# Gated mix of two attentions on one core: small VectorE jobs of slots 1 to 8 handed to GpSimd and ScalarE, the split of the output weights moved

## The chip, the core and the metric

The kernel runs on one core of a Trainium2 chip. The core has five engines that run their own instruction queues in order: TensorE (PE, with its weight loads as PEld), VectorE (DVE), ScalarE (ACT), GpSimd (POOL) and SyncE (SP), whose queue here issues nearly all DMAs. They meet at semaphores alone. The metric is the device time of one launch in microseconds (us), the median of several runs.

## The reference, cut to what matters

One input x (2048 rows of 512) goes through two attention blocks of 32 heads, 16 wide. Block A is causal within four segments of 512 rows, with a memory that is carried from segment to segment; block B is a full softmax attention over all 2048 rows. A gate from x mixes their outputs row by row.

```python
# A, segment s of 4 (L = 512), per head; g = sigmoid(beta)
p = softmax(qs @ ks.T * scale + mask)
o = g * (phi(qs) @ M) / (phi(qs) @ z + 1e-6) + (1 - g) * (p @ vs)
M, z = M + phi(ks).T @ vs, z + phi(ks).sum()
a = concat(o) @ wo
# B
b = concat(softmax(q @ k.T * scale) @ v) @ wo_b
gate = sigmoid((x * gate_w).sum(-1))
out = gate * a + (1 - gate) * b
```

## The kernel before

A first phase (until the first exponential at 341.0 us) projects x to q, k and v of both blocks, works out A's memory part and leaves all of it in DRAM. The second phase is the attention, and the change lies in it.

A *unit* is one block, four heads and 512 query rows: 32 units of A (u = 0 to 31, in the order `UA`) and 32 of B (u = 32 to 63). The loop of line 1050 runs 32 *slots*; slot k treats units ua = k and ub = 32 + k. A slot has 37 *groups* n = 0 to 36 (`NG`): groups 0 to 31 are B's scores, 32 to 36 A's. Two groups make one *iteration* `it` = n // 2, and the work beside the scores hangs on `it`. The schedule is written by hand: each engine takes its instructions in the order in which the program emits them.

In each group:

- `t_group` (583) makes transposed scores, two matmuls (L598) into two of three PSUM banks (`TB`, `MB`), and two exponentials on ScalarE (L604) into `raw`. For A, GpSimd then masks the diagonal blocks (affine selects, L607).
- `plan` puts the *row maxima* of the next slot's B unit (`s_b`, 528: two matmuls L535 and a VectorE maximum over 128 x 1024, L537) beside the groups, one a group, and those of the next A unit (`s_a`, 503: L513, L517, maxima L521 and L523) beside groups 32 to 36. The maxima read the two `sbk` pairs of banks in turn, so TensorE can be two ahead of VectorE and no more.
- `pvs` (965) adds probabilities times values (`pv`, L620) into the bank `PVB`: B's during groups 2 to 33, A's from group 34 to group 0 of the next slot. When a unit is complete, `fin_copy` (623) copies PVB to `pvs` and stores it: B's in group 33 (ScalarE, L629), A's in group 0 of the next slot (VectorE, L627, for u below 31). The first `pv` of B in group 2 waits for that copy.

Other work of a slot:

- `m_chain(k + 1)` (541) at iteration 10 folds the maxima to 128 x 32 numbers (L546) and splits them into a 16-bit and a rest part `m8`. For k + 1 of 8 to 31 GpSimd does the split (L555 to L558), otherwise VectorE (L560 to L562). `m_rows` (564) behind group 24 turns `m8` by TensorE, ScalarE copies it (`mr`), and SP writes it into rows of q that are used from group 32 on and in the next slot.
- `fin_load`, `fin_rec` (641), `fin_bc`: the sums of a finished unit come back from DRAM as `rec`, VectorE takes reciprocals (L644), they are multiplied by the gates, stored (`rd`) and read back as a broadcast `d`. B's `fin_rec` is at iteration 5, A's at 6. The product is VectorE's (L650, L652) for u % 32 below 7 and for 31 and 63, otherwise GpSimd's (L647, L648, L652).
- `fin_norm` (662): GpSimd multiplies 128 x 512 outputs by `d` (L664), B's at iteration 9, A's at 13, in even slots from 2 on.
- `load_wo` (672): in slots 1 to 4 at iteration 9 SP loads a quarter of both output weights and GpSimd splits it (L676 cast, L677 subtraction, twice each).
- From slot 9 on, output rows (`out_rows`, 700) are multiplied in group 1 and later.

Of the kernel before, what the change touches and what calls it, by code (L numbers as in the profile page):

```python
# [38 lines left out]
def gated_mix_kernel(ctx, tc, xt, wq, wk, wv, wo, beta, wqkv, wob, gate_w, out):  # L39
    nc = tc.nc  # L40
# [426 lines left out]
    def load_q(u):  # L467
        kd, qd, c = UN[u]
        load_qk(q_of(u), kd, 0, qd, c)

    def load_ka(u):
        kd, qd, c = UN[u]
        load_qk(KA[u % 2], kd, 1, qd, c)

    def load_kb(k, c=None):
        dst = KB[k % 3] if c is None else KB[k % 3][:, :, c * C:(c + 1) * C]
        load_qk(dst, "B", 1, k % 8, c)
# [6 lines left out]
    def load_vb(g):  # L484
        v_src(VB[g % 2], "B", g % 4, None)

    def load_va(u):
        kd, qd, c = UN[u]
        v_src(VA[(u // 2) % 2], "A", qd // 2, c)
# [4 lines left out]
    def pair_max(k):  # L494
        if k not in MX:
            MX[k] = W.tile([128, 2, 4, 4], FT, name="mx")
        return MX[k]
# [43 lines left out]
    def m_chain(k):  # L541
        mx = pair_max(k)
        if k == 1:
            nc.vector.memset(mx[:, 0], 0.0)
        if k < 32:
            nc.vector.tensor_reduce(mx[:, 1], MXB.pop(32 + k).rearrange("q j p i c -> q (j p) i c"), axis=AX.X,  # L546
                                    op=OP.max)
        else:
            nc.vector.memset(mx[:, 1], 0.0)
        del MX[k]  # L550
        mx = mx.rearrange("q u h i -> q (u h i)")
        m8 = M8[k] = W.tile([128, 2, 32], FT, name="m8")
        hi = W.tile([128, 32], HF, name="mhi")
        if 8 <= k < 32:
            nc.gpsimd.tensor_scalar(mx, mx, -1.0 / AUX, None, op0=OP.mult)  # L555
            nc.gpsimd.tensor_copy(hi, mx)
            nc.gpsimd.tensor_copy(m8[:, 0], hi)
            nc.gpsimd.tensor_tensor(m8[:, 1], mx, hi, op=OP.subtract)  # L558
        else:
            nc.vector.tensor_scalar(hi, mx, -1.0 / AUX, None, op0=OP.mult)  # L560
            nc.vector.tensor_copy(m8[:, 0], hi)
            nc.vector.scalar_tensor_tensor(m8[:, 1], mx, -1.0 / AUX, hi, op0=OP.mult, op1=OP.subtract)  # L562
# [16 lines left out]
    AT = {}  # L579
# [3 lines left out]
    def t_group(u, n, banks, between=()):  # L583


        kd, qd, c = UN[u]
        bs = [bank(banks) for _ in range(2)]
        c0 = 0
        for it, hs in (((n // 2, (n % 2 * 2, n % 2 * 2 + 1)),) if kd == "B" else GA[n]):
            q0 = 128 * it if kd == "A" else 0  # L590
            w = C - q0
            pn = it if kd == "B" else it % 2
            for j, h in enumerate(hs):
                if j:
                    for f in between:
                        f()
                r = slice(64 * j, 64 * j + 64)
                nc.tensor.matmul(bs[j][:, c0:c0 + w], k_of(u, h // 2)[r, 128 * it:128 * it + 128],  # L598
                                 q_of(u)[r, h // 2, q0:], start=True, stop=True)
                PT[u, it, h] = PTILE[pn % 2][:, 2 + j if (kd, it) == ("A", 2) else h][:, c0:c0 + w]  # L600
            c0 += w
        for j in range(2):
            pt = PTILE[pn % 2][:, 2 + j if (kd, n) == ("A", 4) else hs[j]]
            nc.scalar.activation(pt, bs[j], AF.Exp, scale=AT["esc", kd, qd // 2])  # L604
            if kd == "A":
                m = pt[:, :128] if n < 2 else pt.rearrange("p (a t) -> p a t", a=4)[:, ::3 if n < 4 else 2]
                nc.gpsimd.affine_select(out=m, in_=m, pattern=[[1, 128]] if n < 2 else [[0, 2], [1, 128]],  # L607
                                        compare_op=OP.is_ge, fill=0.0, base=0, channel_multiplier=-1)

    def pv(u, it, lo=0, hi=None):  # L610

        kd, qd, c = UN[u]
        g, q = divmod(qd, 2)
        q0 = 128 * it if kd == "A" else 0
        hi = hi or C - q0
        last = 2 if kd == "A" else NT - 1
        vt = VA[(u // 2) % 2] if kd == "A" else VB[g % 2]
        for h in range(4):
            pt = PT[u, it, h]
            nc.tensor.matmul(PVB[32 * h:32 * h + E + 1, q0 + lo:q0 + hi], vt[:, it, 4 * q + h, :], pt[:, lo:hi],  # L620
                             start=it == 0 and lo == 0, stop=it == last and q0 + hi == C, skip_group_check=True)

    def fin_copy(u):

        ps = W.tile([128, C], FT, name="pvs", bufs=1)
        if u < 31:
            nc.vector.tensor_copy(ps, PVB)  # L627
        else:
            nc.scalar.activation(ps, PVB, AF.Copy)  # L629
        AT["pd", u] = D.tile([4, 32, C], FT, name=f"pd{u}")  # L630
        nc.sync.dma_start(AT["pd", u].rearrange("h r t -> (h r) t"), ps)
# [9 lines left out]
    def fin_rec(u):  # L641
        kd, qd, c = UN[u]
        r = AT.pop(("r", u))
        nc.vector.reciprocal(r, r)  # L644
        early = u % 32 < 7 or u in (31, 63)
        if kd == "A" and not early:
            nc.gpsimd.tensor_scalar(r, r, nq[:, qd:qd + 1], None, op0=OP.mult)  # L647
            nc.gpsimd.tensor_tensor(r, r, grow[:, 0, c], op=OP.mult)  # L648
        elif kd == "A":
            nc.vector.scalar_tensor_tensor(r, r, nq[:, qd:qd + 1], grow[:, 0, c], op0=OP.mult, op1=OP.mult)  # L650
        else:
            (nc.vector if early else nc.gpsimd).tensor_tensor(r, r, grow[:, 1, c], op=OP.mult)  # L652
        AT["rd", u] = D.tile([128, E], FT, name=f"rd{u}")
        nc.sync.dma_start(AT["rd", u], r)
# [16 lines left out]

    def load_wo(g):
        for a, w in enumerate((wo, wob)):
            raw = AT["o"][1][:, g, a]
            nc.sync.dma_start(raw, w[g * 128:(g + 1) * 128, :])
            nc.gpsimd.tensor_copy(AT["wh"][:, g, a], raw)  # L676
            nc.gpsimd.tensor_tensor(AT["wl"][:, g, a], raw, AT["wh"][:, g, a], op=OP.subtract)  # L677

    def o_cols(c, t):
        return AT["o"][c % 2][:, :, :, t * 128:(t + 1) * 128]  # L680
# [139 lines left out]
    for n in range(8):  # L820
        w, c = divmod(n, 4)
# [13 lines left out]
    early = st33[:EARLY]  # L835
# [17 lines left out]
    for blk in range(16):  # L853
        g, c = divmod(blk, 4)
# [110 lines left out]
    def pvs(k, n):  # L965

        ua, ub = k, 32 + k
        if n == 0:
            if k:
                pv(ua - 1, 2)  # L970
                fin_copy(ua - 1)
        elif k == 31 and n < 2 * NT:
            if n % 2 and n > 1:
                pv(ub, n // 2 - 1)
        elif 2 <= n < 2 * NT + 2:
            pv(ub, n // 2 - 1, n % 2 * 256, n % 2 * 256 + 256)
            if n == 2 * NT + 1:
                fin_copy(ub)
        elif n > 2 * NT + 1:
            m = n - 2 * NT - 2  # L980
            if m < 2:
                pv(ua, 0, 256 * m, 256 * m + 256)
            else:
                pv(ua, 1)
                pv(ua, 3)
# [64 lines left out]
    for k in range(32):  # L1050
        ua, ub = k, 32 + k
        banks = T3 + [b[:, 0] for b in SBK] * (k == 31)
        for n in range(NG):
            it = n // 2 if n < NG - 1 else NT + 2
            mid = plan.pop((k, n)) if n < 2 * NT and (k, n) in plan else []
            t_group(*(ub, n) if n < 2 * NT else (ua, n - 2 * NT), banks, mid)
            for f in plan.get((k, n), []) + ex[k][0].get(n, []):
                f()
            pvs(k, n)
            for f in ex[k][1].get(n, []):  # L1060
                f()
            if n % 2 == 0 and n < NG - 1:
                continue
            beside(k, it)
            if it == S_LAST:
                m_chain(k + 1)
            if it == 4 and not k:
                late()
            if it == 4 and not k:
                load_q(ub + 2)  # L1070
                for c in range(NC4):
                    load_kb(2, c)
            if it == NT and k < 29:
                load_q(ub + 3)
                load_kb(k + 3)
            if it == 6 and k < 31:
                load_q(ua + 1)
                load_ka(ua + 1)
                if (ua + 1) % 2 == 0:
                    load_va(ua + 1)  # L1080
            if it == 9:
                if k % 2 == 0 and k < 30:
                    load_vb(k // 2 + 1)
                if 1 <= k <= 4:
                    load_wo(k - 1)
    pv(31, 2)
    fin_copy(31)
    fin_bc(63)
# [13 lines left out]
    for t in range(4):  # L1102
        d = den[:, t * 128:(t + 1) * 128]
        o = o_cols(3, t)[:, 3, 0]
# [36 lines left out]
```

## Time and profile before

| what | before |
|---|---|
| median of 3 runs | 1838.19 us (1837.33 to 1839.88) |
| the profiled execution | 1839.64 us, its span 1837.9 us |
| mean granted TensorE clock | 0.997 |
| VectorE's largest group, maxima of B (L537) | 1172.4 us, 1024 times 1.21 us |
| ScalarE's largest, exponentials (L604, tb and mb) | 884.2 + 469.0 us |
| TensorE's largest, probabilities times values of B (L620) | 645.3 us |

The span runs from the first to the last instruction of the profiled execution. Durations of one instruction include a part that overlaps the next one on the same engine, so a sequence is shorter than the sum of its durations; the steps from start to start say what a sequence costs. A row of the timeline has start and length in us, engine, line of the kernel, operation, names, how many instructions were put together, and in brackets the idle time before it with what ended it. The view by stretches gives busy times between two points of the span.

### The profile page before, as it was taken

The numbers are of one execution on the slowest core, as the hardware profiler recorded it, in microseconds if no ns is written. First come the engines' busy times: TensorE is split into PE (matmuls) and PEld (weight loads), VectorE is DVE, ScalarE is ACT, GpSimd is POOL, SyncE is SP. The second block draws the span as 40 slices with busy tenths as digits, with TensorE's granted clock in tenths as the row PEclk, the third lists the DMA queues.
The fourth block names the chain that finished last, engine by engine and source line by source line (L and its number), as shares of the span: only waits on it lengthen the run. The fifth ranks groups of instructions, "written<-read, shape, count | busy, mean of one in ns | idle before, by whom it ended". The sixth has DMA issues, their size and how long they took to land.

```text
span 1837.9 us, 44287 instructions
## 1 busy us (share of the span) xinstructions
PE 1804.9 (98%) x17781; PEld 729.1 (40%) x17781; DVE 1591.5 (87%) x1772; ACT 1432.5 (78%) x2709; POOL 339.6 (18%) x691
## 2 busy tenths in 40 slices
PE   8999999899999999999999999999999999999998
PEld 6787777522222222333333333333333333333325
DVE  7445786699999999999999999999999999999942
ACT  4233333488989999989898989898989898989894
POOL 6100000101212011212121212121212121212122
PEclk9999999999999999999999999999999999999999
DMA  7554534332323232223232323232323232323111
GB/s 231 118 149 124 152 105 108 77 91 73 92 73 91 62 80 62 80 68 86 68 86 68 86 69 85 68 87 68 85 70 87 68 85 70 87 68 86 47 38 61
DMA packets 162482, 158.92 MB, mean 86 GB/s; under 512 B 40140, under 2 KB 126620, under 8 KB 162276
## 3 DMA queue, kind: packets, MB, share of 16 engines
q1 hardware_dynamic: 158692, 149.29, 29.5%
q0 software_dynamic: 3296, 6.27, 1.8%
q8 instruction: 140, 2.29, 0.6%
q14 instruction: 66, 0.54, 0.1%
q10 hardware_dynamic: 288, 0.52, 0.1%
HBM read 103.38 MB, written 50.86 MB: 84 GB/s over the span
## 4 chain that ended last, share of the span: by engine, by line
PE 78%; DVE 15%; ACT 4%; issue 2%; DMA 1%; ACTq 0%; SPq 0%; DVEq 0%; POOLq 0%
PE pvb L620 28%; DVE mxb L537 12%; PE tb L598 12%; PE sbk L535 9%; PE mb L598 6%; PE tb L311 3%; ACT raw L604 3%; PE mb L311 3%; PE tb L705 2%; PE tb L285 2%; PE sbk L513 2%; PE sbk L285 2%; PE sbk L311 1%; PE mb L705 1%; PE pvb L311 1%
## 5 line engine op out<-in xcount | busy, mean ns | idle before, releaser
L537 DVE TENSOR_REDUCE mxb<-sbk 128x2 f32<-128x1024 f32 x1024 | 1172.4, 1210 | 24.7 <-PE sbk L535 13.1
L604 ACT ACTIVATE raw<-tb 128x512 f32<-128x512 f32 x1555 | 884.2, 600 | 63.7 <-PE tb L598 26.9
L620 PE MATMUL pvb<-raw,vb 128*17 128x256 f32 (+1 forms) x8072 | 645.3, 388 | 0.0
L535 PE MATMUL sbk<-kb,qb 64*128 64x512 f16 x2048 | 553.2, 378 | 9.6 <-DVE mxb L537 8.7
L604 ACT ACTIVATE raw<-mb 128x512 f32<-128x512 f32 x782 | 469.0, 600 | 32.7 <-PE mb L598 16.6
L598 PE MATMUL tb<-qb,kb 64*128 64x512 f16 x1342 | 468.2, 381 | 2.0 <-DVE st L326 1.0
L598 PEld LDWEIGHTS <-kb 64*128 64x128 f16 x2048 | 143.3, 93 | 414.8 <-issue 408.9
L620 PEld LDWEIGHTS pvb<-raw,vb 128*17 128x17 f32 x8072 | 138.0, 95 | 403.3 <-issue 393.9
L598 PE MATMUL mb<-qb,kb 64*128 64x512 f16 x679 | 258.6, 381 | 0.0
L607 POOL TENSOR_SCALAR_AFFINE_SELECT raw<-raw 128x256 f32<-128x256 f32 (+1 forms) x320 | 115.4, 361 | 326.4 <-ACT raw L604 318.0
L535 PEld LDWEIGHTS <-qb 64*128 64x128 f16 x2048 | 137.1, 93 | 43.5 <-issue 33.6
L521 DVE TENSOR_REDUCE mx<-sbk 128x2 f32<-128x1024 f32 (+1 forms) x128 | 133.9, 1087 | 7.2 <-PE sbk L517 6.2
L620 PE MATMUL pvb<-raw,va 128*17 128x256 f32 (+2 forms) x1280 | 103.2, 383 | 3.8 <-ACT pvs L629 1.1
L664 POOL TENSOR_TENSOR o<-o,d 128x512 f32<-128x512 f32 x31 | 39.5, 1273 | 218.9 <-DMA d<-rd 176.3
L523 DVE TENSOR_REDUCE mx<-sbk 128x4 f32<-128x512 f32 x64 | 60.5, 946 | 12.4 <-PE sbk L517 12.4
L513 PE MATMUL sbk<-ka,qa 64*128 64x512 f16 (+3 forms) x512 | 70.7, 296 | 0.0
L323 ACT ACTIVATE st<-tb,rng 128x512 f16<-128x512 f32 x25 | 17.2, 688 | 63.4 <-DVE phi L322 25.6
L598 PE MATMUL tb<-qa,ka 64*128 64x512 f16 (+3 forms) x339 | 61.8, 302 | 0.0
L652 POOL TENSOR_TENSOR rec<-rec,grow 128x16 f32<-128x16 f32 x24 | 5.3, 221 | 276.0 <-DVE rec L644 276.0
L517 PE MATMUL sbk<-cmask,crows 64*128 64x64 bf16 x1024 | 52.8, 189 | 0.0
L517 PEld LDWEIGHTS <-crows 64*128 64x128 bf16 x1024 | 46.5, 94 | 13.7
L323 ACT ACTIVATE st<-mb,rng 128x512 f16<-128x512 f32 x21 | 14.4, 687 | 47.6 <-PE mb L311 19.1
(337 smaller groups left out, 1717.0 us busy)
## 6 DMA issues: line engine op xcount, KB each, us to landing
vb<-vdB SPq DMA_DIRECT2D x16, 1088.0 KB
pd<-pvs SPq DMA_DIRECT2D x64, 256.0 KB
kb<-dB SPq DMA_DIRECT2D x60, 256.0 KB
dB<-st SPq DMA_DIRECT2D x64, 128.0 KB
dA<-st SPq DMA_DIRECT2D x64, 128.0 KB
o<-pd SPq DMA_DIRECT2D x64, 128.0 KB
d<-rd SPq DMA_DIRECT2D x63, 128.0 KB
kb<-dB SPq DMA_DIRECT2D x60, 128.0 KB
```

The costliest lines, as they stand in the source:

```text
L285: nc.tensor.matmul(b, (XH, XL)[xi][c][:, n % 4, tl * 128:(tl + 1) * 128], WV[wi][:, n % 4, :], start=n == 0, stop=n == 11)
L311: nc.tensor.matmul(b, WS[ws][w][wi][:, k, :], (XH, XL)[xi][c][:, k, :], start=n == 0, stop=n == 11)
L513: nc.tensor.matmul(b[:, j, c0:c0 + n], q_of(u)[r, p, i * 128:(i + 1) * 128], k_of(u, p)[r, :n], start=True, stop=False)
L517: nc.tensor.matmul(b[:, j, c0 + n - 128 + w.start:c0 + n - 128 + w.stop], crows[r, n2 - 1], cmask[r, n2 - 1, w], start=False, stop=n2 == 2)
L521: nc.vector.tensor_reduce(m[:, :, p, i], b[:, :, :n], axis=AX.X, op=OP.max)
L523: nc.vector.tensor_reduce(m[:, :, :, i], b.rearrange("q j (p k) -> q j p k", p=2)[:, :, :, :n], axis=AX.X, op=OP.max)
L535: nc.tensor.matmul(b[:, j], q_of(u)[r, p, i * 128:(i + 1) * 128], k_of(u, p)[r, kc * C:(kc + 1) * C], start=True, stop=True)
L537: nc.vector.tensor_reduce(MXB[u][:, :, p, i, kc], b, axis=AX.X, op=OP.max)
L598: nc.tensor.matmul(bs[j][:, c0:c0 + w], k_of(u, h // 2)[r, 128 * it:128 * it + 128], q_of(u)[r, h // 2, q0:], start=True, stop=True)
L604: nc.scalar.activation(pt, bs[j], AF.Exp, scale=AT["esc", kd, qd // 2])
L607: nc.gpsimd.affine_select(out=m, in_=m, pattern=[[1, 128]] if n < 2 else [[0, 2], [1, 128]], compare_op=OP.is_ge, fill=0.0, base=0, channe ...
L620: nc.tensor.matmul(PVB[32 * h:32 * h + E + 1, q0 + lo:q0 + hi], vt[:, it, 4 * q + h, :], pt[:, lo:hi], start=it == 0 and lo == 0, stop=it ...
```

## The change

Four edits, all in the second phase:

- `m_chain`: GpSimd splits the maxima for k of 2 to 31 instead of 8 to 31; new are k = 2 to 7, in slots 1 to 6.
- `fin_copy`: ScalarE copies the sums of A's units 0 to 7 too (group 0 of slots 1 to 8).
- `fin_rec`: GpSimd does the gate products for u % 32 of 1 to 6 too (slots 2 to 7, A and B).
- `load_wo` keeps the loads at iteration 9; the GpSimd split becomes `split_wo`, called in the same slots at iteration 14, after that iteration's work from `beside`.

```diff
-        if 8 <= k < 32:
+        if 2 <= k < 32:
             nc.gpsimd.tensor_scalar(mx, mx, -1.0 / AUX, None, op0=OP.mult)
...
         ps = W.tile([128, C], FT, name="pvs", bufs=1)
-        if u < 31:
+        if 8 <= u < 31:
             nc.vector.tensor_copy(ps, PVB)
         else:
             nc.scalar.activation(ps, PVB, AF.Copy)
...
-        early = u % 32 < 7 or u in (31, 63)
+        early = u % 32 < 1 or u in (31, 63)
...
     def load_wo(g):
         for a, w in enumerate((wo, wob)):
+            nc.sync.dma_start(AT["o"][1][:, g, a], w[g * 128:(g + 1) * 128, :])
+
+    def split_wo(g):
+        for a in range(2):
             raw = AT["o"][1][:, g, a]
-            nc.sync.dma_start(raw, w[g * 128:(g + 1) * 128, :])
             nc.gpsimd.tensor_copy(AT["wh"][:, g, a], raw)
             nc.gpsimd.tensor_tensor(AT["wl"][:, g, a], raw, AT["wh"][:, g, a], op=OP.subtract)
...
                 if 1 <= k <= 4:
                     load_wo(k - 1)
+            if it == 14 and 1 <= k <= 4:
+                split_wo(k - 1)
```

## The prediction

> **What bounds the kernel now.** First the page: its span, the busy shares and the chain that ended last.
>
> ```profile
> span 1837.9 us, 44287 instructions
> ...
> PE 1804.9 (98%) x17781; PEld 729.1 (40%) x17781; DVE 1591.5 (87%) x1772; ACT 1432.5 (78%) x2709; POOL 339.6 (18%) x691
> ...
> PE 78%; DVE 15%; ACT 4%; issue 2%; DMA 1%; ACTq 0%; SPq 0%; DVEq 0%; POOLq 0%
> ```
>
> PE looks like the bound, but the ends of its matmuls are modelled, and the share is a mean over all slots. So I cut the trace into slots. ScalarE copies B's sums out of PVB once in each slot, in group 33 of its groups 0 to 36 (the row with L629 below); from one such copy to the next is one slot. The view by stretches gives, from left: stretch, length, then busy time of PE, PEld, DVE, ACT and POOL, the granted clock and the DMA share. The rows are slots 1 to 8.
>
> ```profile
> 396.53:442.31 45.78, 44.25 (x496) 12.95 (x492) 45.09 (x48) 40.80 (x78) 7.30 (x14) 1.00 0.27 74
> 442.31:487.11 44.80, 44.25 (x496) 12.97 (x492) 44.11 (x48) 40.80 (x78) 9.86 (x16) 1.00 0.35 94
> 487.11:534.78 47.67, 45.76 (x496) 13.04 (x492) 45.67 (x48) 40.75 (x77) 7.30 (x14) 0.96 0.27 71
> 534.78:579.58 44.80, 44.25 (x496) 12.97 (x492) 44.12 (x48) 40.60 (x77) 9.86 (x16) 1.00 0.35 94
> 579.58:624.38 44.80, 44.25 (x496) 12.96 (x492) 44.12 (x48) 40.80 (x77) 3.56 (x10) 1.00 0.25 63
> 624.38:669.18 44.80, 44.25 (x496) 12.96 (x492) 44.12 (x48) 40.81 (x78) 6.16 (x13) 1.00 0.31 82
> 669.18:713.45 44.27, 44.04 (x496) 12.96 (x492) 43.65 (x45) 40.68 (x78) 4.59 (x15) 1.00 0.25 64
> 713.45:757.11 43.66, 43.57 (x496) 12.95 (x492) 43.11 (x43) 40.45 (x77) 7.85 (x19) 1.00 0.33 84
> ```
>
> DVE is idle 0.69 us of slot 2 (44.80 - 44.11), 0.62 of slot 7 and 0.55 of slot 8: it sets the pace, and PE's "busy" shrinks and grows with it. What the change asks of slots 1 to 6 can be read off slots 7 and 8, because there the old code already hands over: m_chain goes to POOL from slot 7 on, fin_rec's products from slot 8 on. Slot 7 is 0.53 shorter than slot 6, slot 8 another 0.61 shorter, and DVE got no new idle time. Two slots are out of line: 1 by 0.98 over 44.80 and 3 by 2.87.
>
> **The change part by part.**
>
> *m_chain of 2 to 7 on POOL.* Six slots (1 to 6) at 0.53: **3.2 us**. The four POOL operations delay the m rows no more than in slot 7.
>
> *Products of fin_rec.* Slots 2 to 7, two units in each, 0.61 a slot: **3.7 us**. The store of each product now waits on POOL and holds SP's queue (loads of q, k, v behind it) a little longer, as in slot 8, whose length includes that.
>
> *Output weights no longer split beside m_chain.* Slots 1 and 3 are out of line here. DVE around m_chain in slot 3, POOL's split beside it, and the spread of the two DVE lines (minimum/median/maximum in ns):
>
> ```profile
> 518.67 1.21 DVE L560 TENSOR_SCALAR mhi<-mx 128x32 f16<-128x32 f32 x1
> 519.91 0.52 DVE L561 CAST m<-mhi 128x32 f32<-128x32 f16 x1
> ```
>
> ```profile
> 518.57 1.27 POOL L677 TENSOR_TENSOR wl<-o,wh 128x512 fp32r<-128x512 f32 x1
> ```
>
> ```profile
> L560 DVE TENSOR_SCALAR mhi<-mx x9: 180/181/1205, 313.1 to 1779.2; 128x32 f16<-128x32 f32 x9
> L561 DVE CAST m<-mhi x9: 180/181/523, 313.3 to 1779.4; 128x32 f32<-128x32 f16 x9
> ```
>
> Usually 0.18 each, here 1.21 and 0.52: DVE was held 1.37 us while POOL ran the split. With m_chain on POOL itself, ahead of the split in the same queue, this cannot happen: **0.98 + 1.37 = 2.35 us** back. The other 1.5 us of slot 3's 2.87 is the clock:
>
> ```profile
> 518.50:521.90 3.40, 1.72 (x19) 0.48 (x16) 3.33 (x7) 2.05 (x4) 3.08 (x3) 1.00 0.02 5
> 521.90:525.30 3.40, 3.40 (x27) 0.80 (x24) 2.39 (x3) 1.66 (x4) 0.00 (x0) 0.50 0.00 0
> ...
> 429.80:433.20 3.40, 2.45 (x29) 0.78 (x30) 3.40 (x4) 1.89 (x5) 0.97 (x1) 1.00 0.00 0
> ```
>
> PE starved by that hold was busy 1.72 of 3.40 us, and the next 3.40 us had half the clock. Slot 1's hold left 2.45 busy, and slots 1 and 2 kept 1.00. Without the hold the half clock of slot 3 goes: **1.5 us** back.
>
> *A's sums copied by ScalarE, slots 1 to 8.* The start of slot 2's loop on DVE, then ACT there and around a copy that ACT already makes, then PE (mb and tb are score banks, pvb is PVB):
>
> ```profile
> 447.33 1.23 DVE L537 TENSOR_REDUCE mxb<-sbk 128x2 f32<-128x1024 f32 x1 [0.35 <-PE tb L598]
> 448.47 0.68 DVE L627 COPY pvs<-pvb 128x512 f32<-128x512 f32 x1
> 449.07 2.35 DVE L537 TENSOR_REDUCE mxb<-sbk 128x2 f32<-128x1024 f32 x2
> ```
>
> ```profile
> 447.11 0.60 ACT L604 ACTIVATE raw<-mb 128x512 f32<-128x512 f32 x1 [0.76 <-PE mb L598]
> 447.61 1.26 ACT L604 ACTIVATE raw<-tb 128x512 f32<-128x512 f32 x2
> 448.77 0.59 ACT L604 ACTIVATE raw<-mb 128x512 f32<-128x512 f32 x1
> ```
>
> ```profile
> 487.11 0.60 ACT L629 ACTIVATE pvs<-pvb 128x512 f32<-128x512 f32 x1
> 487.59 0.62 ACT L604 ACTIVATE raw<-mb 128x512 f32<-128x512 f32 x1
> ```
>
> ```profile
> 446.69 0.39 PE L598 MATMUL mb<-qb,kb 64*128 64x512 f16 x1
> ...
> 447.78 0.39 PE L598 MATMUL tb<-qb,kb 64*128 64x512 f16 x1
> ...
> 449.22 0.79 PE L620 MATMUL pvb<-raw,vb 128*17 128x256 f32 x8
> 449.95 0.39 PE L598 MATMUL mb<-qb,kb 64*128 64x512 f16 x1
> ```
>
> Two maxima take 2.35, one 1.22, so they follow every 1.13 us; with the copy between, 449.07 - 447.33 = 1.74. The copy costs DVE 0.61. ACT takes a copy in steps of 0.48 (487.59 - 487.11). Put behind the exponential of 447.61 it starts at 448.09, the next exponentials at 448.57 and 449.05, and the last ends near 449.65 instead of 448.77 + 0.59 = 449.36. The first pv of B needs it (head 3; 449.22 to 450.01 holds a wait for it already), so group 3 starts near 450.25, not 449.95. From a group's first matmul to its maximum is 447.33 - 446.69 = 0.64, so its maximum starts at 450.89. DVE alone would be there at 447.33 + 3 x 1.13 = 450.72: 0.17 is lost once, and afterwards PE's own step of 1.09 (447.78 - 446.69) beats 1.13. I take 0.61 - 0.17 = 0.44, eight slots: **3.5 us**. Bounds: 0.61, and about zero, since the exponentials move by at most ACT's 0.48.
>
> *The split at iteration 14.* POOL runs in program order and nothing ties it to iteration 14. In slots 1 and 3 the split follows m_chain and is over long before the masks of A's scores (affine selects, L607). In slots 2 and 4 the normalisation of A (L664, iteration 13) stands before it and waits for a load of d. POOL, then PE, in slot 2 and POOL in slot 4:
>
> ```profile
> 475.02 0.61 POOL L676 CAST wh<-o 128x512 fp32r<-128x512 f32 x1 [6.16 <-DMA o<-in_A_wo_dram]
> ...
> 477.61 1.27 POOL L677 TENSOR_TENSOR wl<-o,wh 128x512 fp32r<-128x512 f32 x1
> 483.46 1.27 POOL L664 TENSOR_TENSOR o<-o,d 128x512 f32<-128x512 f32 x1 [4.58 <-DMA d<-rd]
> 485.63 0.29 POOL L607 TENSOR_SCALAR_AFFINE_SELECT raw<-raw 128x128 f32<-128x128 f32 x1 [0.90 <-ACT raw L604]
> ...
> 487.29 0.29 POOL L607 TENSOR_SCALAR_AFFINE_SELECT raw<-raw 128x128 f32<-128x128 f32 x1 [0.20 <-ACT raw L604]
> ```
>
> ```profile
> 487.86 0.62 PE L620 MATMUL pvb<-raw,va 128*17 128x256 f32 x8
> ```
>
> ```profile
> 575.46 1.27 POOL L664 TENSOR_TENSOR o<-o,d 128x512 f32<-128x512 f32 x1 [2.39 <-DMA d<-rd]
> 578.11 0.29 POOL L607 TENSOR_SCALAR_AFFINE_SELECT raw<-raw 128x128 f32<-128x128 f32 x1 [1.38 <-ACT raw L604]
> ```
>
> The split takes 477.61 + 1.27 - 475.02 = 3.86. Behind the normalisation it ends at 484.73 + 3.94 = 488.67, and the first mask starts at 488.75, not 485.63. Four in a row at 0.37 end at 490.15 instead of 487.58. The fourth head of A's first pv (487.86) needs the fourth: PE stands for 2.3 us. In slot 4 the normalisation ends at 576.73, the masks start at 580.75 instead of 578.11, 0.5 less: 1.9 us. Behind the pv in PE's order are A's last score groups and maxima, and DVE is already waiting for PE as the next slot opens (0.35 at 447.33), so nothing hides it: **-4.2 us**. Bounds: 0 (d lands 3 us sooner) and the whole 3.9 a slot.
>
> *Clock after these holds.* 2.3 us without matmuls leave a 3.4 us window with little more than 1.1 busy, under the 1.72 that halved the clock, unless the window's edge cuts the hold. I count it for both, at slot 3's price: **-3.0 us** (bounds 0 and -3.4, half of two windows).
>
> Sum: 3.2 + 3.7 + 2.35 + 1.5 + 3.5 - 4.2 - 3.0 = 7.0 us gained. The profiled execution took 1839.64 us (1.7 outside its span), 1.45 above the median shown, within the three runs' spread. So 1832.6 for it, **1831.2** for the median of 1838.19.
>
>
> **The rivals.**
> 1. *Holds, but no half clock.* The window's edge cuts both holds, or the 1.72 was not the cause. Speaks for it: one case only. Gain 10.0: 1828.2. The Trainium skill (TensorE: Matmul & The Clock Gate, Part 1) would have the clock fall only after a whole idle window, which gives this rival; the window of 1.72 above does not agree.
> 2. *ACT pushes PE as much as DVE gains.* ACT is busy 40.8 of 44.8, so its slack is thin between groups. Copy worth nothing: gain 3.5, 1834.7.
> 3. *Nothing held*, d there early or the pv covered: gain 14.2, 1824.0. Against it: d landed late in both slots.
> 4. *Masks held by the whole 3.9 twice and the copy worth nothing*: 7.0 - 3.5 - 3.6 = -0.1, 1838.3, no change.
> 5. *The hand-over gains nothing*: PE and SP wait for POOL's slower operations on m and the products as long as DVE saves. The first two terms go: gain 0.1, 1838.1. Against it: slots 7 and 8 got shorter by 0.53 and 0.61 by just this. The Trainium skill (GPSIMD Engine Reference, section 4.1 Engine selection) is on this rival's side: elementwise work belongs to VectorE, and GpSimd is about half as fast at it. Slots 7 and 8 do not agree, VectorE being the one that is full.
> 6. *Slower: the clock stays down after the holds.* 1.5 us lost per 3.4 at half clock is 0.44 per us; the gain is gone and 3.7 more after 24 us of extra half clock. Two stretches of 20 us instead of 3.4 cost 14.6: 1845.8. Against it: slot 3's half clock ended after 3.4 us.
>
> **How the numbers follow.** Forecast 0.46; rivals 1 to 6: 0.20, 0.13, 0.08, 0.04, 0.03, 0.06. About 0.2% (3.7 us) can be told from no change. Faster: 0.46 + 0.20 + 0.08 + half of rival 2, 0.80; same 0.14; slower 0.06. The range 1825.5 to 1836.0 takes in the forecast and rivals 1 and 2 (0.79) with edges of the others.
>
> **What would show it.** Slots by the same copies: 43.8, 43.2, 47.1, 43.2, 46.6, 43.2, 43.2, 43.2. DVE lines 560 and 561 gone in slots 1 to 6; L644 alone left of the products; L607 after L677 in slots 2 and 4, PE waiting on it; clock 0.96 in slots 3 and 5 from such waits. Wrong if slots 3 and 5 are near 43.2, if DVE gets idle time in groups 2 to 6 of each slot, or if a later slot changes.

## The result

| | median | runs |
|---|---|---|
| before | 1838.19 us | 1836.94 to 1839.88, 5 runs |
| changed | 1828.94 us | 1827.88 to 1830.10, 5 runs |

The ratio of changed to before is 0.9949, with a 95% interval of 0.9934 to 0.9964: the change gains 9.25 us, where 7.0 were forecast. The profiled executions stand further apart, 1839.64 against 1828.94 us, because the one of before lay above its median. Experiments 1 to 4 and 5 to 8 come from two later groups of runs, in which the kernel before measured 1838.39 and 1837.75 us. Each ratio below is to the kernel before in its own group; a distance from the changed kernel crosses groups, so some half a microsecond of it means nothing.

### The profile page after: what moved, and what is told of

It is laid out like the page before. It is cut to its first block, busy times and chain, and to the rows that moved or that the text cites. A ratio compares the mean times of both kernels' runs of the same rounds, so it can differ in the third digit from the quotient of the medians.

```text
span 1827.2 us, 44300 instructions
## 1 busy us (share of the span) xinstructions
PE 1796.1 (98%) x17781; PEld 726.1 (40%) x17781; DVE 1579.1 (86%) x1734; ACT 1431.4 (78%) x2717; POOL 348.8 (19%) x733
## 4 chain that ended last, share of the span: by engine, by line
PE 86%; DVE 6%; ACT 4%; issue 2%; DMA 1%; POOL 0%; ACTq 0%; SPq 0%; DVEq 0%; POOLq 0%
PE pvb L620 32%; PE tb L598 13%; PE sbk L535 11%; PE mb L598 7%; DVE mxb L537 4%; ACT raw L604 3%; PE tb L311 3%; PE mb L311 3%; PE tb L708 2%; PE tb L285 2%; PE sbk L513 2%; PE sbk L285 2%; PE sbk L311 1%; PE mb L708 1%; PE pvb L311 1%
## 5 line engine op out<-in xcount | busy, mean ns | idle before, releaser
L535 PE MATMUL sbk<-kb,qb 64*128 64x512 f16 x2048 | 558.8, 378 | 4.5 <-DVE mxb L537 4.4
L598 PEld LDWEIGHTS <-kb 64*128 64x128 f16 x2048 | 139.6, 93 | 414.5 <-issue 410.5
L535 PEld LDWEIGHTS <-qb 64*128 64x128 f16 x2048 | 133.3, 93 | 32.3 <-issue 20.8
```

The source lines that it names most:

```text
L535: nc.tensor.matmul(b[:, j], q_of(u)[r, p, i * 128:(i + 1) * 128], k_of(u, p)[r, kc * C:(kc + 1) * C], start=True, stop=True)
```

## The profile after

The page of the changed kernel, span and busy shares:

```profile
span 1827.2 us, 44300 instructions
...
PE 1796.1 (98%) x17781; PEld 726.1 (40%) x17781; DVE 1579.1 (86%) x1734; ACT 1431.4 (78%) x2717; POOL 348.8 (19%) x733
```

PE's share has not moved. Slots 1 to 8 by stretches, cut at the same copies of B's sums (stretch, length, busy time of PE, PEld, DVE, ACT, POOL, granted clock, DMA share, GB/s):

```profile
396.91:440.81 43.90, 43.44 (x496) 12.43 (x492) 43.16 (x44) 40.81 (x79) 8.18 (x18) 1.00 0.28 77
440.81:484.06 43.25, 42.93 (x496) 12.48 (x492) 42.62 (x42) 40.57 (x79) 9.35 (x19) 1.00 0.36 97
484.06:528.91 44.85, 43.65 (x496) 12.75 (x492) 42.80 (x42) 40.58 (x79) 10.80 (x25) 1.00 0.28 75
528.91:572.15 43.24, 42.92 (x496) 12.54 (x492) 42.61 (x42) 40.48 (x79) 9.63 (x20) 1.00 0.36 98
572.15:616.68 44.53, 43.68 (x496) 12.72 (x492) 42.79 (x42) 40.34 (x79) 6.86 (x21) 1.00 0.25 63
616.68:659.92 43.24, 42.92 (x496) 12.47 (x492) 42.61 (x42) 40.56 (x78) 7.84 (x19) 1.00 0.33 85
659.92:703.16 43.24, 42.92 (x496) 12.49 (x492) 42.62 (x42) 40.57 (x78) 5.30 (x17) 1.00 0.25 66
703.16:746.41 43.25, 42.93 (x496) 12.47 (x492) 42.63 (x42) 40.57 (x79) 7.85 (x19) 1.00 0.32 85
```

The whole gain is in these rows. They add up to 349.50 us against 360.58, 11.1 less; slot 0 ended 0.38 later, and from the end of slot 8 to the last copy of B's sums both kernels take 1049.57 us. Forecast and measured stand close in six slots: 43.8 and 43.90 in slot 1, 43.2 and 43.24 or 43.25 in slots 2, 4, 6, 7 and 8. Slots 3 and 5 are longer than these, but by 1.6 and 1.3 us where 3.9 and 3.4 were expected, and their clock is 1.00.

GpSimd, then TensorE, at the end of slot 2 (start, length, engine, line, how many, and in brackets the idle time before):

```profile
480.31 1.27 POOL L664 TENSOR_TENSOR o<-o,d 128x512 f32<-128x512 f32 x1 [7.86 <-DMA d<-rd]
481.53 0.61 POOL L679 CAST wh<-o 128x512 fp32r<-128x512 f32 x1
482.22 1.27 POOL L680 TENSOR_TENSOR wl<-o,wh 128x512 fp32r<-128x512 f32 x1
483.44 0.61 POOL L679 CAST wh<-o 128x512 fp32r<-128x512 f32 x1
484.13 1.27 POOL L680 TENSOR_TENSOR wl<-o,wh 128x512 fp32r<-128x512 f32 x1
485.35 1.75 POOL L607 TENSOR_SCALAR_AFFINE_SELECT raw<-raw 128x128 f32<-128x128 f32 x6
```

```profile
484.48 0.24 PE L517 MATMUL sbk<-cmask,crows 64*128 64x64 bf16 x4
485.69 1.34 PE L620 MATMUL pvb<-raw,va 128*17 128x256 f32 x8 [0.97 <-ACT raw L604]
486.97 0.33 PE L598 MATMUL tb<-qa,ka 64*128 64x384 f16 x1
```

The normalisation waits for d, the split for the normalisation, the masks for the split, A's first pv for the masks: the first mask starts at 485.35, 1.29 after the slot's cut, where it stood 1.48 ahead of the cut before (485.63 against 487.11). The bracket names ACT as what pv waited for; the exponentials of these four heads had ended by 484.17, and each head's mask ends 0.05 us ahead of its first matmul. Waiting masks run without a gap: four of 128x128 at steps of 0.24 and two of 128x256 behind them, six in 1.75 us. By the modelled ends TensorE is without a matmul only for the 0.97 in the bracket (0.62 at the end of slot 4); the rest of the hold lies inside the pv row, which takes 1.34 us where it took 0.62 before, since each head runs as its own mask ends.

The starts of slot 2's loop on VectorE and ScalarE:

```profile
445.83 5.93 DVE L537 TENSOR_REDUCE mxb<-sbk 128x2 f32<-128x1024 f32 x5 [0.35 <-PE tb L598]
```

```profile
446.11 0.59 ACT L604 ACTIVATE raw<-tb 128x512 f32<-128x512 f32 x1
446.58 0.60 ACT L629 ACTIVATE pvs<-pvb 128x512 f32<-128x512 f32 x1
447.06 0.62 ACT L604 ACTIVATE raw<-tb 128x512 f32<-128x512 f32 x1
447.54 0.63 ACT L604 ACTIVATE raw<-mb 128x512 f32<-128x512 f32 x1
```

The copy sits in ScalarE's row at steps of 0.48, as the one of group 33 did. Five maxima take 5.93 us; at 1.13 a step with the last one whole (4 x 1.13 + 1.22) they would take 5.74. The 0.19 is what ScalarE's copy takes back (experiment 3 shows the row without it).

## The experiments

Each edit is shown against the changed kernel, or against another one where the text says so. "Slots" are cut as above.

### 1. The split ahead of A's normalisation

```diff
-            if it == 14 and 1 <= k <= 4:
+            if it == 11 and 1 <= k <= 4:
                 split_wo(k - 1)
```

> The changed kernel with the split of the output weights at iteration 11 instead of 14, so that GpSimd has it behind m_chain and ahead of the normalisation of A. Theory (the split behind the normalisation holds A's masks in slots 2 and 4, and that is all that makes slots 3 and 5 longer than their neighbours, 44.85 and 44.53 against 43.24): slots 3 and 5 fall to 43.24, slot 1 and the rest stay, the time is 2.9 us below the changed kernel's 1828.9: 1826.0. Rival (the slots are longer for another reason, the split's reads or the loads of the weights): slots 3 and 5 stay at 44.5 to 44.9, 1828.9.

Measured: 1825.56 us (1825.22 to 1829.48), ratio to before 0.9931 (0.9914 to 0.9947). Slots 2 to 5 by stretches, and GpSimd in slot 2:

```profile
444.24:487.49 43.25, 42.93 (x496) 12.47 (x492) 42.62 (x42) 40.56 (x78) 11.55 (x23) 1.00 0.35 97
487.49:530.74 43.25, 42.93 (x496) 12.48 (x492) 42.62 (x42) 40.58 (x78) 8.95 (x21) 1.00 0.29 78
530.74:573.99 43.25, 42.93 (x496) 12.53 (x492) 42.62 (x42) 40.49 (x78) 11.56 (x23) 1.00 0.36 98
573.99:617.28 43.29, 42.97 (x496) 12.44 (x492) 42.62 (x42) 40.35 (x79) 5.30 (x17) 1.00 0.26 65
```

```profile
480.42 1.28 POOL L680 TENSOR_TENSOR wl<-o,wh 128x512 fp32r<-128x512 f32 x1
483.60 1.27 POOL L664 TENSOR_TENSOR o<-o,d 128x512 f32<-128x512 f32 x1 [1.91 <-DMA d<-rd]
486.01 0.29 POOL L607 TENSOR_SCALAR_AFFINE_SELECT raw<-raw 128x128 f32<-128x128 f32 x1 [1.14 <-ACT raw L604]
```

The split is over before d lands, the masks wait for exponentials alone, and slots 3 and 5 are like their neighbours. The order on GpSimd was all that made them longer; the theory holds, and the median is 3.4 us under the changed kernel's. The intervals of the two ratios overlap; slots 1 to 8 of the profiles are 2.85 us shorter, and the rest is within the spread.

### 2. Maxima split by VectorE again

```diff
-        if 2 <= k < 32:
+        if 8 <= k < 32:
             nc.gpsimd.tensor_scalar(mx, mx, -1.0 / AUX, None, op0=OP.mult)
```

> The changed kernel with the maxima of units 2 to 7 split by VectorE again; the output weights' split stays at iteration 14. Theory (what freed slots 1 and 3 from the stretched VectorE operations is that GpSimd itself now splits the maxima ahead of the output weights; iteration 14 alone ties GpSimd to nothing there): L560 and L561 are again stretched to about 0.8 to 1.2 and 0.5 us in slots 1 and 3, these are longer than the changed kernel's by 0.53 + 1.0 and 0.53 + 1.4 us, slots 2, 4, 5 and 6 by 0.53, and a half clock may follow in slot 3 (1.5 more). Sum 3.2 + 2.4 = 5.6 us, 1834.5, with the half clock 1836.0. Rival (moving the split to iteration 14 keeps it clear of m_chain by itself): L560 and L561 stay at 0.18, 0.53 in each of six slots, 3.2 us, 1832.1.

Measured: 1836.11 us (1830.87 to 1840.81, ten runs), ratio to before 0.9989 (0.9978 to 0.9999). In its profile slots 1 to 6 take 45.44, 43.78, 46.17, 43.78, 45.01 and 43.78 us: 0.48 to 0.54 more than the changed kernel in slots 2, 4, 5 and 6, 1.54 and 1.32 more in slots 1 and 3. Slot 1, VectorE and GpSimd:

```profile
429.38 0.90 DVE L560 TENSOR_SCALAR mhi<-mx 128x32 f16<-128x32 f32 x1
430.31 0.52 DVE L561 CAST m<-mhi 128x32 f32<-128x32 f16 x1
430.75 0.18 DVE L562 SCALAR_TENSOR_TENSOR m<-mx,mhi 128x32 f32<-128x32 f32 x1
430.85 3.47 DVE L537 TENSOR_REDUCE mxb<-sbk 128x2 f32<-128x1024 f32 x3
```

```profile
428.27 0.61 POOL L679 CAST wh<-o 128x512 fp32r<-128x512 f32 x1 [25.52 <-DVE mxb L537]
428.96 1.27 POOL L680 TENSOR_TENSOR wl<-o,wh 128x512 fp32r<-128x512 f32 x1
430.19 0.60 POOL L679 CAST wh<-o 128x512 fp32r<-128x512 f32 x1
430.87 1.26 POOL L680 TENSOR_TENSOR wl<-o,wh 128x512 fp32r<-128x512 f32 x1
```

The split is emitted at iteration 14 here, but GpSimd, with nothing ahead of it, starts it beside m_chain of iteration 10, and the two VectorE operations are stretched again. L560 ends with GpSimd's subtraction (430.28 and 430.23), L561 with its cast (430.83 and 430.79); the three maxima beside the next subtraction keep their step of 1.13. In slot 3 the two operations take 1.08 and 0.52, 1.24 more than their usual 0.18 each, and the hold by the masks is 0.4 shorter than in the changed kernel (d landed 0.43 earlier, seen from the slot's end): with the 0.53 that makes about the 1.32. So the maxima's move to GpSimd freed slots 1 and 3, not iteration 14. The Trainium skill (SBUF — State Buffer, section Who interferes with whom) says that VectorE's copies, casts and tensor_scalar can take a port pair that GpSimd needs, whole instruction by whole instruction, and that tensor_reduce never does; the rows agree, though these maxima read PSUM and so test the second half only for that. The half clock that the expectation allows for is not in this profile (1.00 in slot 3). The ten runs spread over 10 us, more than those of the other kernels, and the granted clock goes with it, from 0.999 in the fastest (1830.87) to 0.994 in the slowest (1840.81); so the median says less here than the slots.

### 3. A's sums copied by VectorE again

```diff
-        if 8 <= u < 31:
+        if u < 31:
             nc.vector.tensor_copy(ps, PVB)
```

> The changed kernel with A's sums of units 0 to 7 copied by VectorE again. Theory (the copy is worth 0.42 to 0.44 a slot, 0.61 less what ScalarE's copy costs TensorE at the slot's start): slots 1 to 8 each 0.42 longer, 3.4 us, 1832.3, slots 3 and 5 perhaps less, being held by TensorE there. Rival (worth its whole 0.61 on VectorE): 4.9 us, 1833.8; rival (worth nothing, other parts gave what was put down to it): 1828.9.

Measured: 1832.64 us (1831.49 to 1836.03), ratio to before 0.9968 (0.9958 to 0.9978), 3.7 us over the changed kernel. Slots 2, 4, 6, 7 and 8 take 43.67, each 0.42 or 0.43 more, slot 1 0.37 more. Slot 3 takes 44.81 and slot 5 45.26, 0.04 less and 0.73 more: the holds there are not the same in every execution (experiment 7 says what they follow). With the copy on VectorE, the four maxima behind it take 4.61 us, which is 3 x 1.13 + 1.22: no step is lost there. The copy is worth 0.42, its 0.61 less the 0.19 that ScalarE's copy takes back, as worked out.

### 4. The split at iteration 9

```diff
                     load_wo(k - 1)
+                    split_wo(k - 1)
-            if it == 14 and 1 <= k <= 4:
-                split_wo(k - 1)
```

> The changed kernel with the split of the output weights at iteration 9 behind its loads, as in the kernel before, so that the maxima's split on GpSimd comes behind it. Theory (GpSimd takes its queue in order, so m is late by what is left of the 3.9 us of split when the maxima are ready): the matmuls of m_rows stand some 1.7 us in slots 1 and 3 and some 4 us in slots 2 and 4, where the weights land late; VectorE loses about 0.4 less each, 1.3 and 3.6; a hold of 4 us leaves one window nearly without matmuls, so that a half clock follows (1.5 each); A's masks are free again (2.9 back). Sum 2.6 + 7.2 + 3.0 - 2.9 = 9.9 us over the changed kernel, 1838.8. Rival (m has room enough until group 24, as in later slots): only the masks come free, 1826.0. Rival (hold, but no half clock): 1835.8.

Measured: 1847.13 us (1846.70 to 1849.93), ratio to before 1.0048 (1.0031 to 1.0065). Slots 1 to 4 take 46.01, 51.45, 45.36 and 51.14 us. TensorE in slot 2, then two stretches of 3.4 us around the end of its wait:

```profile
478.39 0.63 PE L620 MATMUL pvb<-raw,vb 128*17 128x256 f32 x8
484.82 0.84 PE L568 MATMUL tb<-ident,m 128*32 128x128 f32 x4 [5.80 <-POOL m L557]
485.59 0.60 PE L598 MATMUL mb<-qb,kb 64*128 64x512 f16 x1
```

```profile
479.50:482.90 3.40, 0.00 (x0) 0.00 (x0) 0.58 (x1) 0.00 (x0) 2.76 (x4) 0.99 0.01 3
482.90:486.30 3.40, 1.48 (x8) 0.50 (x8) 0.00 (x0) 0.34 (x2) 1.85 (x5) 0.50 0.00 0
```

The mechanism holds and its size was too small, 9.9 us over the changed kernel expected and 18.2 measured: the split began 3.5 us after m_chain's reduction (L546, 476.48; the cast at 479.98) where it was 1.4 in the kernel before (473.62, 475.02), and TensorE waited 5.8 us instead of 4 in slot 2; slots 1 and 3 lost 2.1 instead of 1.3. Behind each of the long waits the clock is at 0.50 for 6.8 us. With the maxima on GpSimd, leaving the split where it was would have made the kernel slower than before.

### 5. Two quarters of the split in one slot

```diff
-            if it == 14 and 1 <= k <= 4:
-                split_wo(k - 1)
+            if it == 14 and k in (2, 4):
+                split_wo(k - 2)
+                split_wo(k - 1)
```

> The changed kernel with the splits of slots 1 and 2 both in slot 2, those of slots 3 and 4 both in slot 4, at iteration 14. Theory (A's masks wait for the whole split that stands ahead of them on GpSimd, and a window of 3.4 us of which TensorE is busy 0.53 or less brings half clock): masks and first pv of A 3.9 us later still, so slots 3 and 5 hold 1.6 + 3.9 and 1.3 + 3.9 us over 43.25, and about 2 us more each for half clock, as behind the 6 us holds of the kernel with the split at iteration 9: 50.7 and 50.4; the other slots stay at 43.25; 11.7 us over the changed kernel, 1840.6. Rival (no half clock behind masks that are late): 7.7 us, 1836.6. Rival (half of the hold was the load of d, not the split): under 6 us, below 1835.

Measured: 1839.46 us (1839.12 to 1842.74), ratio to before 1.0013 (1.0004 to 1.0022), 10.5 us over the changed kernel. Slots 3 and 5 take 49.83 and 49.47 us, slot 1 43.85, the others 43.25. Three stretches around the end of slot 2:

```profile
484.71:488.12 3.41, 1.41 (x24) 0.68 (x16) 3.00 (x3) 2.34 (x5) 3.25 (x5) 1.00 0.29 103
488.12:491.53 3.41, 0.64 (x4) 0.40 (x6) 0.00 (x0) 0.00 (x0) 3.33 (x8) 0.50 0.87 171
491.53:494.94 3.41, 3.41 (x29) 1.06 (x26) 1.16 (x1) 1.09 (x2) 1.58 (x5) 0.50 0.57 138
```

Slot 3 holds 6.6 us over 43.25: 1.6 as in the changed kernel, 3.8 for the second quarter, and 1.2 that is left for the half clock. Twice the split, twice the delay, and now the clock falls too. The price was put at 2 us; part of the half clock passed while TensorE had little to do (0.64 of 3.41 us in the second row). The expectation counted on half clock behind a window with 0.53 or less; here the one ahead of it has 1.41.

### 6. ScalarE copies all of A's sums

Against the kernel of experiment 1:

```diff
-        if 8 <= u < 31:
+        if u < 0:
             nc.vector.tensor_copy(ps, PVB)
```

> The kernel with the split at iteration 11, and ScalarE copies all of A's sums, in slots 9 to 31 too. Theory (the copy gains only where VectorE works without a gap behind it; from slot 9 on VectorE waits for TensorE at groups 1 and 2 anyway, 0.34 and 0.89 us in slot 10, because of the output rows): slots 9 to 31 stay at 45.68 to 45.82, the time at 1825.6. Rival (0.42 in each of these slots too): 22 x 0.42 = 9.2 us less, 1816.4. Rival (ScalarE's copy delays the exponentials, and TensorE, which is the bound at group 1 there, with them): up to 0.3 a slot more, 1832.

Measured: 1826.47 us (1826.11 to 1826.94), ratio to before 0.9938 (0.9923 to 0.9953): no gain over experiment 1. From the end of slot 8 to the last copy of B's sums it takes 1049.89 us, against 1049.47 there. VectorE at the start of slot 10, in experiment 1 and here:

```profile
797.80 1.23 DVE L537 TENSOR_REDUCE mxb<-sbk 128x2 f32<-128x1024 f32 x1 [0.35 <-PE tb L598]
798.94 0.68 DVE L627 COPY pvs<-pvb 128x512 f32<-128x512 f32 x1
799.97 1.23 DVE L537 TENSOR_REDUCE mxb<-sbk 128x2 f32<-128x1024 f32 x1 [0.34 <-PE sbk L535]
```

```profile
793.99 1.23 DVE L537 TENSOR_REDUCE mxb<-sbk 128x2 f32<-128x1024 f32 x1 [0.35 <-PE tb L598]
796.14 1.23 DVE L537 TENSOR_REDUCE mxb<-sbk 128x2 f32<-128x1024 f32 x1 [0.93 <-PE sbk L535]
```

From the first maximum to the second it is 2.17 with the copy and 2.15 without: the 0.59 of the copy became idle time. From slot 9 on, TensorE's output rows are late at this place, and VectorE's copy lay in the wait for them.

### 7. Gate products by VectorE again

```diff
-        early = u % 32 < 1 or u in (31, 63)
+        early = u % 32 < 7 or u in (31, 63)
```

> The changed kernel with the gate products of units 1 to 6 of A and B by VectorE again. Theory (they cost VectorE 0.61 a slot in slots 2 to 7 and GpSimd nothing that counts): these slots 0.61 longer, 3.7 us, 1832.6. Rival (GpSimd's products are late for the normalisations and part of slots 3's and 5's hold): slots 3 and 5 are no longer or shorter, under 2.5 us, 1831.4.

Measured: 1832.41 us (1831.61 to 1833.26), ratio to before 0.9970 (0.9958 to 0.9982), 3.5 us over the changed kernel. Slots 2, 4, 6 and 7 take 0.61 or 0.62 more, slot 5 0.60, slot 3 only 0.17. The hold follows d: the later d lands, the longer the slot behind it, one for one. A's normalisation starts as d lands; the hold is what the slot has over its neighbours.

| kernel | start ahead of the end of slot 2 | hold in slot 3 | ahead of the end of slot 4 | hold in slot 5 |
|---|---|---|---|---|
| changed | 3.75 | 1.60 | 4.10 | 1.29 |
| experiment 3 | 4.21 | 1.14 | 3.75 | 1.59 |
| experiment 7 | 4.20 | 1.16 | 4.11 | 1.28 |

In each pair, start and hold add up to 5.34 to 5.39. Experiment 3 leaves the products on GpSimd and has both the early d and the late one, so the products are not what makes slot 3 differ; why d lands when it does was not followed.

### 8. The last products handed over too

Against the kernel of experiment 1:

```diff
-        early = u % 32 < 1 or u in (31, 63)
+        early = u in (31, 63)
```

> The kernel with the split at iteration 11, and GpSimd makes the gate products of units 0 of A and B as well, in slot 1, the only slot that still had them on VectorE. Theory: slot 1 goes from 43.85 to 43.25, all slots 1 to 8 are alike, 0.6 us less than 1825.6: 1825.0. Rival (slot 1 is longer because its loads arrive late): 43.85 stays, 1825.6.

Measured: 1825.73 us (1825.34 to 1826.30), ratio to before 0.9933 (0.9919 to 0.9946). Slots 1 and 2:

```profile
396.54:439.78 43.24, 42.92 (x496) 12.47 (x492) 42.61 (x42) 40.57 (x78) 8.97 (x21) 1.00 0.28 78
439.78:483.03 43.25, 42.94 (x496) 12.48 (x492) 42.62 (x42) 40.57 (x78) 11.58 (x23) 1.00 0.36 97
```

Slot 1 is 0.6 shorter and like the rest, as the theory has it. The medians of experiments 1 and 8 do not show 0.6 us: slot 0 ended at 396.54 in this profile and at 400.39 in that of experiment 1, and such differences of the first phase cover it. Both versions are faster than the kernel before. Every run of this one lies below every run of the changed kernel (1827.88 and more); of experiment 1, one run of four (1829.48) lies among them.

## Why the prediction was near, and where it was off

| step | forecast | measured | from |
|---|---|---|---|
| maxima on GpSimd, six slots | 3.2 | 0.48 to 0.54 a slot, 3.2 | experiment 2, slots 2, 4, 5, 6 |
| gate products, six slots | 3.7 | 0.61 a slot, 3.7 | experiment 7, slots 2, 4, 6, 7 |
| VectorE no longer stretched, slots 1 and 3 | 2.35 | 1.0 and 1.2 | experiment 2, slot 1 beyond 0.53, slot 3 by L560 and L561 |
| A's sums by ScalarE, eight slots | 3.5 | 0.42 a slot, 3.4 | experiment 3 |
| masks held behind the split | -4.2 | -1.6 and -1.3, 2.9 in all | slots 3 and 5 against experiment 1 |
| half clock gone from slot 3 | 1.5 | gone, clock 1.00 | slot 3 after |
| half clock behind the new holds | -3.0 | 0 | slots 3 and 5 after |

The bound was read rightly: VectorE works nearly without a gap, and what it no longer has to do comes off the slot nearly whole. The stretched operations were put down to the split beside them; experiment 2 brought them back by moving m_chain alone. What they cost differs with where the two meet, 1.37 us in slot 3 of the profile before and 1.24 in experiment 2.

The step that failed is "Clock after these holds". I took 2.3 us without matmuls for certain and a window with some 1.1 busy. The changed kernel has 0.97 us without matmuls in slot 2 and 0.62 in slot 4, because A's first pv does not wait for its fourth mask as a whole: it starts behind the first mask and goes on head by head. The window around it, cut within 0.1 us of the edges on which the clock records change, and the next one:

```profile
484.87:488.28 3.41, 2.59 (x30) 1.10 (x32) 2.20 (x3) 1.59 (x4) 2.38 (x8) 1.00 0.60 178
488.28:491.70 3.42, 3.42 (x49) 1.48 (x46) 2.86 (x3) 2.58 (x6) 1.47 (x4) 1.00 0.96 190
```

2.59 busy of 3.41, and the clock stays. That is the first rival's outcome, though not for its reason: an edge may cut the 0.97, but a window that held all of it would still be some 2.4 busy, well above 1.72.

The term before it was right in its mechanism and mis-sized: 2.3 and 1.9 us forecast, 1.6 and 1.3 measured. The forecast gave each waiting mask 0.37 us; they follow at 0.24, so that the fourth ends 0.38 us sooner. It let the masks start 5.29 us behind the start of the normalisation (488.75 - 483.46), and they start 5.04 behind it (485.35 - 480.31), each operation beginning just before the end of the one ahead. With d 0.1 earlier in slot 2, seen from the slot's end, that is the 0.7 us by which its hold was put too high. In slot 4, where d landed as in the kernel before, it is the 0.6 without that 0.1.

With the holds at 2.9 and no half clock the same sum gives 11.35, against 11.1 in the slots. The medians are only 9.25 apart, because the profiled execution of before, from which the terms come, lay 1.45 over its median, and slot 0 ended 0.38 later in the changed kernel. The half clock in slot 3 of that execution cost about as much as the 1.45; that the median execution had none there was not shown. So the forecast of 7.0 was near in part by luck: it charged 4.3 us too much for the holds and the clock, and some 2 us of its gains did not reach the medians.

## What to carry to other kernels

Before handing an engine's work to another one, read the receiving queue in program order: here a split put behind an operation that waits for a load held up masks that TensorE needed, and three iterations earlier it cost nothing. An iteration in the program is no time: in experiment 2 GpSimd had nothing ahead of the split of iteration 14 and ran it beside m_chain of iteration 10. Work taken from a full engine is worth something only where that engine has no idle time behind it: 0.42 us a slot for the copy in slots 1 to 8, nothing from slot 9 on.

## What the runs showed of the hardware

The clock fell behind windows that were far from idle. By the windows of 3.41 us on whose edges the clock records change, half clock followed 1.72 us of matmuls (slot 3 before) and 1.41 (experiment 5), and not the 2.59 above nor this one of experiment 4:

```profile
530.62:534.03 3.41, 1.83 (x18) 0.63 (x20) 1.56 (x2) 1.17 (x4) 1.51 (x5) 1.00 0.00 0
534.03:537.44 3.41, 3.41 (x40) 0.74 (x36) 3.41 (x4) 3.33 (x7) 0.00 (x0) 1.00 0.08 17
```

In these rows the edge lies near half busy, between 1.72 and 1.83 of 3.41, with ends of matmuls that are modelled. Other windows of the traces blur it: half clock followed 1.81 in experiment 3 (338.54 to 341.96) and, in the kernel before, a window that reads as busy throughout (71.37 to 74.79, mostly matmuls with a 128x1 operand), while full clock followed one of 1.53 shortly before that kernel's end (1832.65 to 1836.06). So no threshold is shown, only that a window need not be without matmuls for the clock to fall. The Trainium skill (TensorE: Matmul & The Clock Gate, Part 1) lets the clock fall after a window that was idle; in slot 3 before and in experiment 5 the window ahead of the half clock was not idle.
